# Transposed probabilities stored by 64-query halves: which engine copies what, and into which range

## The chip, the cores and the metric

The kernel runs on one core of one Trainium2 chip. The metric is the device time of one execution in microseconds. It is one hand-scheduled program that runs attention, a mixture-of-experts layer and a second feed-forward layer one after the other.

## The reference

Only the first part, attention, is touched by the change. Everything is float32; B = 2 batches, H = 8 heads, S = 576 positions, D = 64.

```python
scores = scale * np.matmul(q, k.transpose(0, 1, 3, 2))
...
scores = scores + bias.transpose(2, 0, 1)[None, :, :, :]   # a small network of the distance
scores = scores - np.max(scores, axis=-1, keepdims=True)
attn = np.exp(scores)
attn = attn / (np.sum(attn, axis=-1, keepdims=True) + 1e-09)
return np.matmul(attn, v).astype(np.float32)
...
x = np.ascontiguousarray(attn_out.transpose(0, 2, 1, 3)).reshape(B * S, H * D)
x = _moe_ref(x=x, **moe_kwargs)      # each token goes to one of 8 experts, weighted by its gate
return _moe2_ref(x=x, **moe2_kwargs) # 512 -> 2048 -> 512 with a leaky activation
```

## The kernel before, in words

**Units and slots.** Heads are taken in pairs `hp` (0 to 3). The 576 queries are cut into four blocks of 128 and a rest of 64. `SL` lists 24 slots: slots 0 to 3 hold the rests ("small" units) of batch 0, slots 4 to 11 one block each of batch 0, and from slot 12 on a slot holds a unit of two blocks (0 and 1, or 2 and 3) of one head pair; slots 12, 13, 18 and 20 hold a small unit of batch 1 besides. Slots 14 to 17 are batch 0, blocks 2 and 3; slot 18 begins the second half of batch 1. Slot 24 only finishes slot 23's unit.

**The course.** Slot s computes the scores of its own unit u = SL[s] and finishes the unit w = SL[s - 1] of the slot before. TensorE, ScalarE and VectorE follow the order in which `course` writes their instructions. SyncE's transfers (SP) are ordered by a scheduler, each as early as its buffer comes free. For two-block units the order is: scores of u's first block (TensorE, L253); `low`, which adds the bias, takes the minimum of the negated sum and writes it to SBUF (VectorE, L260, twice, one per head); the transposes of w's probabilities (`turn`, L290) with their copies to SBUF; the exponentials of u's first block (`expo`, ScalarE, L267, one per head, each followed by a read of its accumulator); scores and `low` of u's second block; if the slot before held a small unit, that one's transposes; `values`, the products with the values (L330, and L332 for the last 64 keys); the exponentials of the second block; the copy of the products to `xT` (VectorE, L334).

**Transposes and copies.** Nine column groups j of 128 hold the two heads' 1152 probabilities of a query: 0 to 3 for one head, 5 to 8 for the other, 4 the last 64 of both. `turn(w, 4)`, `turn(w, 0, 1, 2, 3)` and `turn(w, 5, 6, 7, 8)` each transpose their groups into one PSUM tile of two banks: the two 64-query halves of a block go to bank 0 and bank 1 (TensorE works on both halves of its rows). The copy function that `turn` returns, called with `('A')`, lets ScalarE copy both banks (L274); with `('A', 'D')` ScalarE copies bank 0 and VectorE bank 1 (L276). Their target is the SBUF tile `PT` [128, 9, 256]: for each j, 256 columns ordered (block, half, query), so the two engines' 64-column runs alternate. Where two instructions of different engines write overlapping ranges of a tile, the second waits for the first. PSUM holds two such tiles of two banks ("pt", also used by `values`, `row` and the routing) and two for the scores ("pq"); a tile is written again only when its readers are done.

**`row`.** From slot 17 on, steps of the routing of batch 0 are woven in. `row(0, 1)` and `row(3, 4)` transpose two blocks of finished rows (L478) into one two-bank tile, multiply each by the reciprocal sums (VectorE, L488) and append its gate and index (L489); GpSimd then scatters them. The first row's transposes come first, then its multiplication, then the second row's. `row(2)` stands alone.

**After attention** (from about 193 us): the two feed-forward parts, TensorE's stream of matmuls on split float32 weights.

Of the kernel before, what the change touches and what calls it, by code (L numbers as in the profile page):

```python
# [10 lines left out]
F32 = mybir.dt.float32  # L11
# [10 lines left out]
B, H, S, D = 2, 8, 576, 64  # L22
# [17 lines left out]
def build(tc, nc, a):  # L40
    V, A, G, T, SY = nc.vector, nc.scalar, nc.gpsimd, nc.tensor, nc.sync
    with contextlib.ExitStack() as ctx:
# [8 lines left out]
        ap = pool(left, "ap", 2)  # L51
# [5 lines left out]
        packed = True  # L57
        ps2 = lambda name: pt.tile([128, 2, 512], F32, tag="pt", name=name)

        def ps1(p, name):  # L60
            if packed:
                return ps2(name)[:, 0]
            return p.tile([128, 512], F32, tag="pt" if p is pt else "pa", name=name)
# [34 lines left out]
        ident = gp.tile([128, 128], F32, name="ident")  # L98
# [8 lines left out]
        xT = [xp.tile([128, 4, 640], F32, tag=f"xT{b}", name=f"xT{b}") for b in range(B)]  # L107
# [123 lines left out]
        halfs = [slice(64 * h, 64 * h + 64) for h in range(2)]  # L231
# [32 lines left out]
        def expo(u, ul=0, h=0):  # L264

            out, mn, acc = u.sc[ul, h]
            A.activation(out, out, AF.Exp, bias=mn, scale=-1.0, accum_out=acc)  # L267
            if u.small:
                u.dup = ap.tile([128, 2, 64], F32, tag="dup", name="dup", bufs=2)
                G.tensor_copy(u.dup, u.P[:, 512:576].unsqueeze(1).to_broadcast([128, 2, 64]))  # L270
# [7 lines left out]
        def turn(u, *js):  # L278

            t = ps2("t1")  # L280
            if u.small:
                u.PT = ap.tile([128, 5, 128], F32, tag="pt4", name="pt4", bufs=2)
                rows = [u.P[:, 128 * j:128 * j + 128] for j in range(4)] + [u.dup.rearrange("p a b -> p (a b)")]
            else:
                if js[0] == u.first:
                    u.PT = ap.tile([128, 9, 256], F32, tag="PT", name="PT")
                rows = [u.P[ul][:, 128 * j:128 * j + 128] for j in js for ul in u.uls]
            for i, x in enumerate(rows):
                for h, p in enumerate(halfs):
                    T.transpose(t[:, h, 64 * i:64 * i + 64], x[p], ident[p, p])  # L290
            src = t[:, :, 0:64 * len(rows)].rearrange("p h (m c) -> p h m c", c=64)
            if u.small:
                def out():
                    copy('A', u.PT[:, 0:4].rearrange("p m (h c) -> p h m c", h=2), src[:, :, 0:4])
                    for h, p in enumerate(halfs):
                        copy('D', u.PT[p, 4, 0:64], src[p, h, 4])
                return out
            dst = u.PT[:, js[0]:js[-1] + 1, :128 * len(u.uls)]
            if len(u.uls) == 2:
                dst = dst.rearrange("p j (i h c) -> p h (j i) c", h=2, c=64)  # L300
            else:
                dst = dst.rearrange("p j (h c) -> p h j c", h=2)

            def out(*es):
                if len(es) == 1:
                    copy(es[0], dst, src)
                else:
                    for h, e in enumerate(es):
                        copy(e, dst[:, h], src[:, h])
            return out  # L310

        def values(*us):
            o = ps1(pa, "av")
            outs, at = [], 0
            for u in us:
                v = u.v
                if u.small:
                    n, dst = 64, xT[u.b][:, u.hp, 512:576]
                    rhs = lambda h, j: u.PT[:, j, 64 * h:64 * h + 64]
                    rest = u.PT[:, 4, 0:64]  # L320
                else:
                    n, q0 = 128 * len(u.uls), 128 * u.uls[0]
                    dst = xT[u.b][:, u.hp, q0:q0 + n]
                    rhs = lambda h, j: u.PT[:, 5 * h + j, :n]
                    rest = u.PT[:, 4, :n]
                c = slice(at, at + n)
                at += n
                for j in range(4):
                    for h, p in enumerate(halfs):
                        T.matmul(o[p, c], v[:, j, p], rhs(h, j), start=j == 0, stop=False, skip_group_check=True)  # L330
                for p in halfs:
                    T.matmul(o[p, c], vd[u.b][:, u.hp, p], rest, start=False, stop=True, skip_group_check=True)  # L332
                outs.append((dst, o[:, c]))
            return lambda: [V.tensor_copy(*z) for z in outs]  # L334

        def first(f):
# [31 lines left out]
        def routing(b):  # L368
# [100 lines left out]

            def row(*us):  # L470
                t = ps2("xp") if packed else ps1(pt, "xp")
                for i, u in enumerate(us):
                    x = r.x[u] = raw.tile([128, RW], F32, tag="xr", name="xr", bufs=5)
                    if packed:
                        c = 256 * i
                        for hp in range(4):
                            for h, p in enumerate(halfs):
                                T.transpose(t[:, h, c + 64 * hp:c + 64 * hp + 64], xT[b][p, hp, 128 * u:128 * u + 128],  # L478
                                            ident[p, p])
                        z = x[:, 0:DM].rearrange("p (g h d) -> p h g d", h=2, d=64)  # L480
                        y = t[:, :, c:c + 256].rearrange("p h (g d) -> p h g d", d=64)
                        w = r.rinv[:, u].rearrange("p (g h) -> p h g", h=2).unsqueeze(3).to_broadcast([128, 2, 4, 64])
                    else:
                        for hp in range(4):
                            T.transpose(t[:, 128 * hp:128 * hp + 128], xT[b][:, hp, 128 * u:128 * u + 128], ident)
                        z, y = [z.rearrange("p (h d) -> p h d", h=8) for z in (x[:, 0:DM], t)]
                        w = r.rinv[:, u].unsqueeze(2).to_broadcast([128, 8, 64])
                    V.tensor_tensor(z, y, w, ALU.mult)  # L488
                    V.tensor_copy(x[:, DM:RW], r.gt[:, u])  # L489
# [428 lines left out]
        def course():  # L918
# [51 lines left out]
            for s in range(NU + 1):  # L970
# [11 lines left out]
                if u is None or len(u.uls) == 2:  # L982
# [3 lines left out]
                        low(u, u.uls[0], 1)  # L986
                    if len(w.uls) == 2:
                        turn(w, 4)('A')
                        if u:
                            expo(u, u.uls[0], 0)  # L990
                        turn(w, 0, 1, 2, 3)('A', 'D')
                        turn(w, 5, 6, 7, 8)('A', 'D')
                    else:
                        turn(w, 0, 1, 2, 3, 4)('A')
                        expo(u, u.uls[0], 0)
                        turn(w, 5, 6, 7, 8)('A')
                    if u:
                        scores(u, u.uls[1])
                        expo(u, u.uls[0], 1)
                        low(u, u.uls[1], 0)  # L1000
                        low(u, u.uls[1], 1)
# [246 lines left out]
```

## Time and profile before

| | us |
|---|---|
| time before, median of 3 runs | 386.43 (385.21 to 387.69) |
| profiled execution, its own time | 386.03 |
| its span, first to last instruction | 384.1 |
| TensorE matmuls busy | 351.6 |
| VectorE busy | 279.3 |
| ScalarE busy | 233.6 |
| first and last start of VectorE's copies to PT (L276) | 92.8, 186.7 |

The table's busy times are unions over the whole span; TensorE's is modelled, since its matmuls are pipelined. Times in rows of the trace are from the span's start. A row "x8" stands for eight instructions merged; a bracket gives the engine's idle time just before and what ended it.

### The profile page before, as it was taken

The page shows a single profiled execution, that of the slowest core. Times are in us where ns is not written, and L with a number is a line of the kernel's source. Part 1 is how long each engine was busy: PE and PEld are TensorE (multiplying, and loading weights), DVE is VectorE, ACT ScalarE, POOL GpSimd, SP SyncE. Part 2 cuts the span into 40 slices and gives each one's busy share as a digit, 9 for nine tenths or more (in the row PEclk, how much of TensorE's full clock was granted, in tenths as well). Part 3 has the DMA queues.
Part 4 walks back from the last instruction along what each step waited for, and adds up shares of the span by engine and source line. Part 5 has one row for each costly group of instructions (what it writes and reads, how often), then busy time and mean ns, then how long its engine had stood idle before and what let it go on. Part 6 is the DMA issues. An engine that isn't in the chain of part 4 may idle for free. (4 is left out here: it accounts for less than half of the span.)

```text
span 384.1 us, 8342 instructions
## 1 busy us (share of the span) xinstructions
PE 351.6 (92%) x3132; PEld 264.0 (69%) x3133; DVE 279.3 (73%) x679; ACT 233.6 (61%) x518; POOL 29.2 (8%) x48
## 2 busy tenths in 40 slices
PE   4988999999999998888799979999999999999992
PEld 2423565666666656565479979778988989887881
DVE  5988977846656656877589996048999999678430
ACT  4877899987656654555663446236776675555531
POOL 2000000000000000023013330020000000000013
PEclk9999999999999999999999999999999999999997
DMA  8897987999999940610883695863566556340003
GB/s 317 226 302 258 381 276 245 295 287 342 335 375 388 390 183 20 215 57 18 276 220 119 185 300 189 265 199 95 159 190 182 173 178 180 118 132 2 1 0 136
DMA packets 44013, 78.82 MB, mean 205 GB/s; under 512 B 7127, under 2 KB 21591, under 8 KB 43964
## 3 DMA queue, kind: packets, MB, share of 16 engines
q1 hardware_dynamic: 42780, 75.73, 61.0%
q0 software_dynamic: 1184, 2.48, 1.8%
q8 instruction: 26, 0.43, 0.5%
q14 instruction: 23, 0.19, 0.1%
HBM read 59.50 MB, written 20.09 MB: 207 GB/s over the span
## 5 line engine op out<-in xcount | busy, mean ns | idle before, releaser
L267 ACT ACTIVATE p<-p,mn 128x576 f32<-128x576 f32 x72 | 56.0, 778 | 20.2 <-DVE mn L260 20.2
L260 DVE CUSTOM_DVE_ANT_0 p<-sps,bias 128x576 f32<-128x576 f32 x72 | 51.9, 754 | 19.3 <-PE sps L253 12.0
L253 PE MATMUL sps<-kqv 64*128 64x288 f32 x256 | 50.7, 429 | 2.5 <-DVE mn L260 1.9
L176 DVE TENSOR_SCALAR h<-c 128x528 f32<-128x528 f32 (+17 forms) x126 | 46.5, 445 | 0.2
L184 PE MATMUL bps<-h,c 128*32 128x512 f32 (+17 forms) x352 | 36.5, 503 | 7.6 <-DVE h L176 5.2
L253 PEld LDWEIGHTS sps<-kqv 64*128 64x128 f32 x256 | 28.3, 186 | 15.8 <-DVE mn L260 5.0
L274 ACT COPY PT<-t 128x512 f32<-128x512 f32 (+2 forms) x52 | 26.8, 549 | 19.4 <-PE t L290 19.4
L330 PE MATMUL av<-PT,kqv 128*64 128x256 f32 (+1 forms) x320 | 35.5, 344 | 2.1 <-DVE PT L276 1.2
L851 PE MATMUL fg<-yh,w1l 128*128 128x304 f32 x120 | 36.3, 302 | 0.0
L851 PE MATMUL fg<-yh,w1h 128*128 128x304 f32 x120 | 36.2, 302 | 0.0
L851 PE MATMUL fg<-yl,w1h 128*128 128x304 f32 x120 | 36.2, 302 | 0.0
L290 PEld LDWEIGHTS t<-ident,p 64*128 64x128 f32 x640 | 28.9, 139 | 10.5 <-DVE PT L276 2.7
L290 PE MATMUL t<-ident,p 64*128 64x64 f32 x640 | 32.9, 227 | 2.9 <-DVE xT L334 1.2
L192 ACT ACTIVATE st<-bps,c 128x527 f32<-128x527 f32 (+35 forms) x72 | 31.1, 510 | 4.4 <-PE bps L184 4.4
L776 ACT ACTIVATE cv<-d 128x512 f32<-128x512 f32 x32 | 21.6, 674 | 19.7 <-DMA d<-in_wout 11.2
L330 PEld LDWEIGHTS av<-PT,kqv 128*64 128x64 f32 x320 | 20.8, 136 | 17.7 <-DVE PT L276 6.4
L863 PE MATMUL facc<-w2h,hl 128*128 128x512 f32 (+1 forms) x75 | 30.1, 401 | 0.3 <-DVE hl L547 0.3
L863 PE MATMUL facc<-w2h,hh 128*128 128x512 f32 (+1 forms) x75 | 29.8, 397 | 0.4 <-ACT hh L546 0.3
L863 PE MATMUL facc<-w2l,hh 128*128 128x512 f32 (+1 forms) x75 | 29.6, 394 | 0.0
L184 PEld LDWEIGHTS bps<-h,c 128*32 128x32 f32 x352 | 12.2, 115 | 23.6 <-DVE mn L260 8.9
L546 ACT CAST hh<-g 128x304 fp32r<-128x304 f32 x32 | 14.3, 445 | 15.9 <-DVE g L855 15.9
L851 PEld LDWEIGHTS fg<-yh,w1h 128*128 128x128 f32 x120 | 22.6, 188 | 1.0
(200 smaller groups left out, 735.2 us busy)
## 6 DMA issues: line engine op xcount, KB each, us to landing
bias<-bd SPq DMA_DIRECT2D x24, 576.0 KB, 6.5
kqv<-in_kqv SPq DMA_DIRECT2D x14, 864.0 KB, 7.7
bd<-st SPq DMA_DIRECT2D x36, 295.5 KB, 6.3
raw<-in_ew SPq DMA_DIRECT2D x16, 512.0 KB, 6.5
d<-in_win SPq DMA_DIRECT2D x16, 512.0 KB, 3.9
d<-in_wout SPq DMA_DIRECT2D x16, 512.0 KB, 3.5
w<-in_ew SPq DMA_DIRECT2D x6, 512.0 KB, 8.4
xd<-zr SPq DMA_DIRECT2D x4, 722.8 KB, 12.4
```

The lines of the kernel that those rows point to most:

```text
L176: V.tensor_scalar(h, tab[:, :n], psi[:, i:i + 1], 0.0, ALU.add, ALU.max)
L184: T.matmul(ps[32 * c:32 * c + 32, n0:n1], w2n, hs[c][:, n0:n1], start=True, stop=True)
L192: A.activation(st[:, o:o + src.shape[1]], src, AF.Copy, scale=rr[:, t:t + 1])
L253: T.matmul(u.sc[ul, h][0][:, nh, :288], q[p, 128 * ul:128 * ul + 128], k[p, 288 * nh:288 * nh + 288], start=True, stop=True)
L260: V.tensor_tensor_reduce(out.rearrange("p (a b) -> p a b", a=2), ps[:, :, :288], bias.rearrange("p (a b) -> p a b", a=2), -0.125, 3.0e38, ...
L267: A.activation(out, out, AF.Exp, bias=mn, scale=-1.0, accum_out=acc)
L274: A.copy(o, i)
L290: T.transpose(t[:, h, 64 * i:64 * i + 64], x[p], ident[p, p])
L330: T.matmul(o[p, c], v[:, j, p], rhs(h, j), start=j == 0, stop=False, skip_group_check=True)
L776: A.mul(v, r[:, :, 1].bitcast(F32), 2.0 ** -112)
L851: T.matmul(ps, w[:, 128 * k:128 * k + 128], x[:, k, s], start=k + i == 0, stop=k + i == 5)
L863: T.matmul(acc[i][:m], h[:, r:r + m], w, start=f == 0 and j == 0, stop=f == NF - 1 and j == 2)
```

## The change

1. `PT` becomes [128, 2, 9, 128]: half first, then j, then (block, query). Each half's copy fills a range of its own.
2. `values` reads its moving operand as two pieces, one per half; its output columns come in the order (half, block, query), and the copy to `xT` puts them back.
3. In two-block slots the copy of groups 0 to 3 goes to ScalarE whole instead of being split, and the first exponential moves behind all the copies. In slot 12 (one-block w) the exponential moves behind the second copy.
4. In `row`, the transposes of both rows come before both multiplications.

```diff
--- before.py
+++ after.py
@@ -283,7 +283,7 @@
                 rows = [u.P[:, 128 * j:128 * j + 128] for j in range(4)] + [u.dup.rearrange("p a b -> p (a b)")]
             else:
                 if js[0] == u.first:
-                    u.PT = ap.tile([128, 9, 256], F32, tag="PT", name="PT")
+                    u.PT = ap.tile([128, 2, 9, 128], F32, tag="PT", name="PT")
                 rows = [u.P[ul][:, 128 * j:128 * j + 128] for j in js for ul in u.uls]
             for i, x in enumerate(rows):
                 for h, p in enumerate(halfs):
@@ -295,11 +295,8 @@
                     for h, p in enumerate(halfs):
                         copy('D', u.PT[p, 4, 0:64], src[p, h, 4])
                 return out
-            dst = u.PT[:, js[0]:js[-1] + 1, :128 * len(u.uls)]
-            if len(u.uls) == 2:
-                dst = dst.rearrange("p j (i h c) -> p h (j i) c", h=2, c=64)
-            else:
-                dst = dst.rearrange("p j (h c) -> p h j c", h=2)
+            dst = u.PT[:, :, js[0]:js[-1] + 1, :64 * len(u.uls)]
+            src = src.rearrange("p h (j i) c -> p h j (i c)", i=len(u.uls))
 
             def out(*es):
                 if len(es) == 1:
@@ -321,8 +318,8 @@
                 else:
                     n, q0 = 128 * len(u.uls), 128 * u.uls[0]
                     dst = xT[u.b][:, u.hp, q0:q0 + n]
-                    rhs = lambda h, j: u.PT[:, 5 * h + j, :n]
-                    rest = u.PT[:, 4, :n]
+                    rhs = lambda h, j: u.PT[:, :, 5 * h + j, :n // 2]
+                    rest = u.PT[:, :, 4, :n // 2]
                 c = slice(at, at + n)
                 at += n
                 for j in range(4):
@@ -330,7 +327,11 @@
                         T.matmul(o[p, c], v[:, j, p], rhs(h, j), start=j == 0, stop=False, skip_group_check=True)
                 for p in halfs:
                     T.matmul(o[p, c], vd[u.b][:, u.hp, p], rest, start=False, stop=True, skip_group_check=True)
-                outs.append((dst, o[:, c]))
+                y = o[:, c]
+                if not u.small:
+                    y, dst = [z.rearrange(r, c=64, i=len(u.uls))
+                              for z, r in ((y, "p (h i c) -> p h i c"), (dst, "p (i h c) -> p h i c"))]
+                outs.append((dst, y))
             return lambda: [V.tensor_copy(*z) for z in outs]
 
         def first(f):
@@ -469,16 +470,17 @@
 
             def row(*us):
                 t = ps2("xp") if packed else ps1(pt, "xp")
+                if packed:
+                    for i, u in enumerate(us):
+                        for hp in range(4):
+                            for h, p in enumerate(halfs):
+                                c = 256 * i + 64 * hp
+                                T.transpose(t[:, h, c:c + 64], xT[b][p, hp, 128 * u:128 * u + 128], ident[p, p])
                 for i, u in enumerate(us):
                     x = r.x[u] = raw.tile([128, RW], F32, tag="xr", name="xr", bufs=5)
                     if packed:
-                        c = 256 * i
-                        for hp in range(4):
-                            for h, p in enumerate(halfs):
-                                T.transpose(t[:, h, c + 64 * hp:c + 64 * hp + 64], xT[b][p, hp, 128 * u:128 * u + 128],
-                                            ident[p, p])
                         z = x[:, 0:DM].rearrange("p (g h d) -> p h g d", h=2, d=64)
-                        y = t[:, :, c:c + 256].rearrange("p h (g d) -> p h g d", d=64)
+                        y = t[:, :, 256 * i:256 * i + 256].rearrange("p h (g d) -> p h g d", d=64)
                         w = r.rinv[:, u].rearrange("p (g h) -> p h g", h=2).unsqueeze(3).to_broadcast([128, 2, 4, 64])
                     else:
                         for hp in range(4):
@@ -986,15 +988,13 @@
                         low(u, u.uls[0], 1)
                     if len(w.uls) == 2:
                         turn(w, 4)('A')
-                        if u:
-                            expo(u, u.uls[0], 0)
-                        turn(w, 0, 1, 2, 3)('A', 'D')
+                        turn(w, 0, 1, 2, 3)('A')
                         turn(w, 5, 6, 7, 8)('A', 'D')
                     else:
                         turn(w, 0, 1, 2, 3, 4)('A')
-                        expo(u, u.uls[0], 0)
                         turn(w, 5, 6, 7, 8)('A')
                     if u:
+                        expo(u, u.uls[0], 0)
                         scores(u, u.uls[1])
                         expo(u, u.uls[0], 1)
                         low(u, u.uls[1], 0)
```

## Rows read from the trace of the kernel before

**Rows 1.** The page's busy time, share of the span and instructions, TensorE.

```profile
PE 351.6 (92%) x3132; PEld 264.0 (69%) x3133; DVE 279.3 (73%) x679; ACT 233.6 (61%) x518; POOL 29.2 (8%) x48
```

**Rows 2.** Waits, 88 to 192 us: engine, line, waited for: us, times, longest.

```profile
DVE PT L276 <- ACT PT L274: 8.8, 12, 0.8
...
PEld av L330 <- DVE PT L276: 6.4, 14, 0.7
```

**Rows 3.** Timeline around a `row` pair: start, us, engine, line, operation.

```profile
167.60 0.33 PEld L478 LDWEIGHTS xp<-ident,xT 64*128 64x128 f32 x8 [1.00 <-DVE xr L488]
...
169.13 0.76 DVE L260 CUSTOM_DVE_ANT_0 p<-sps,bias 128x576 f32<-128x576 f32 x1
```

**Rows 4.** Timeline of a plain slot (16, from 113.61) and the next starts.

```profile
114.69 1.47 PE L290 MATMUL t<-ident,p 64*128 64x64 f32 x36
...
115.01 0.37 ACT L274 COPY PT<-t 128x256 f32<-128x256 f32 x1 [1.36 <-PE t L290]
...
115.57 0.75 DVE L260 CUSTOM_DVE_ANT_0 p<-sps,bias 128x576 f32<-128x576 f32 x1
...
115.75 0.78 ACT L267 ACTIVATE p<-p,mn 128x576 f32<-128x576 f32 x1 [0.36 <-DVE mn L260]
...
115.99 1.63 PE L253 MATMUL sps<-kqv 64*128 64x288 f32 x8
...
116.52 1.05 ACT L274 COPY PT<-t 128x512 f32<-128x512 f32 x2
...
117.12 1.29 DVE L276 COPY PT<-t 128x512 f32<-128x512 f32 x2 [0.79 <-ACT PT L274]
...
117.87 2.32 PE L330 MATMUL av<-PT,kqv 128*64 128x256 f32 x15 [0.25 <-DVE PT L276]
...
118.46 1.27 PEld L330 LDWEIGHTS av<-PT,kqv 128*64 128x64 f32 x13 [0.41 <-DVE PT L276]
...
119.95 0.76 ACT L267 ACTIVATE p<-p,mn 128x576 f32<-128x576 f32 x1
...
120.03 0.80 PE L332 MATMUL av<-PT,vd 128*64 128x256 f32 x3
...
120.76 0.79 PEld L253 LDWEIGHTS sps<-kqv 64*128 64x128 f32 x8 [0.38 <-issue]
...
127.92 0.79 PEld L253 LDWEIGHTS sps<-kqv 64*128 64x128 f32 x8 [0.39 <-issue]
```

**Rows 5.** Groups by shape: count, busy us, mean ns, idle before.

```profile
L274 ACT COPY PT<-t 128x512 f32<-128x512 f32 x32 | 17.4, 580 | 0.8 <-PE t L290 0.8
...
L276 DVE COPY PT<-t 128x512 f32<-128x512 f32 x24 | 15.5, 686 | 8.8 <-ACT PT L274 8.8
...
L274 ACT COPY PT<-t 128x640 f32<-128x640 f32 x8 | 5.5, 694 | 4.0 <-PE t L290 4.0
```

**Rows 6.** Timeline of slot 14, which has a small unit to finish.

```profile
102.98 0.33 PEld L290 LDWEIGHTS t<-ident,p 64*128 64x128 f32 x8 [0.68 <-DVE PT L276]
103.58 1.95 PE L330 MATMUL av<-PT,kqv 128*64 128x256 f32 x16
105.36 0.60 PE L332 MATMUL av<-PT,vd 128*64 128x256 f32 x4
```

**Rows 7.** Timeline, products of a one-block unit.

```profile
75.40 1.09 PE L330 MATMUL av<-PT,kqv 128*64 128x128 f32 x16
```

**Rows 8.** Timeline, slots 19 and 24.

```profile
145.18 1.52 PEld L330 LDWEIGHTS av<-PT,kqv 128*64 128x64 f32 x16 [0.59 <-ACT p L267]
...
186.80 0.36 PEld L599 LDWEIGHTS xjT<-ident,xj 96*128 96x128 f32 x4 [1.04 <-DVE PT L276]
```

**Rows 9.** Windows: busy us (x) of each engine, clock, DMA share, GB/s.

```profile
86.00:140.00 54.00, 51.52 (x564) 33.31 (x565) 32.37 (x86) 34.41 (x83) 1.22 (x5) 1.00 1.00 360
140.00:150.00 10.00, 9.17 (x131) 7.30 (x127) 7.10 (x22) 5.08 (x12) 0.22 (x1) 1.00 0.01 2
```

**Rows 10.** DMA issues within 113.2 to 113.6: KB, us to landing.

```profile
kqv<-in_kqv SPq DMA_DIRECT2D x1, 864.0 KB, 12.1
```

## The prediction

> **What bounds the kernel now.** I began with the busy line of the page: TensorE is busy 92% of the span, the next engine far less [rows 1], so time is won where TensorE stands still, or streams behind a wait. The view of waits, cut to the stretch of the two-block units, names who makes it wait: the products with the values (L330) wait for VectorE's copies of the transposed probabilities (L276) 14 times, 6.4 us; those copies had themselves waited 12 times, 8.8 us, for ScalarE's copy of the other half [rows 2]. Twice, the transposes of `row` wait for the multiplication of the row before, L488 [rows 3]. Then I read one plain slot in order of time [rows 4]; the reader should lay its rows side by side. VectorE ends the last `low` of the first block at 116.33 (115.57 + 0.75, plus 0.08 to read the accumulator) and is idle until 117.12, which is when ScalarE's first copy ends (116.52 + about 0.58 [rows 5]). The two copies fill different 64-column groups of one range, and have different source banks; nothing else links them. ScalarE in turn spent 115.75 to 116.52 on an exponential that nobody needs before the next slot. So PT is full only at 118.41, the scores of the second block have ended at 117.62, two weight loads of L330 go at 117.87, and the other eighteen of its and L332's twenty from 118.46. The slot lasts 7.15 us (113.61 to 120.76, 120.76 to 127.92 [rows 4]).
>
> **Part 1: the copies of j = 0 to 3 go to ScalarE whole, ahead of the exponential.** A plain slot, step by step. The 36 transposes start at 114.69 and end at 116.16, about 0.04 us each; the twentieth, the last that this copy needs, ends near 115.5. ScalarE is free of the j = 4 copy at 115.38. The trace has no 1024-element copy; 512 elements take 0.580 and 640 take 0.694 us [rows 5], 0.89 ns per element, which gives 1.04 us; its bounds are 0.94 (two copies back to back take 1.05 [rows 4], so the second adds 0.47; twice that) and 1.16 (two whole ones). So it runs 115.55 to 116.6, and ScalarE's half of j = 5 to 8 ends near 117.1. VectorE's only copy, its half of j = 5 to 8, starts when `low` is done and its transposes are: 116.4 to 117.1. PT is full at 117.1 instead of 118.41, before the scores of the second block end at 117.62. What is late next is TensorE itself: L330 starts when those scores have ended. At the other boundary of the slot the same is seen: the last L332 product ends at 120.83 and the first weight load of the next scores goes at 120.76, after 0.38 us in which nothing was waited for [rows 4]. I take 117.55 for the first weight load. Uninterrupted, the twenty products take 2.38 us (103.58 to 105.96, in a slot where they start with everything ready [rows 6]), so they end at 119.93 instead of 120.83: **0.9 us**. If instead the eighteen keep the pace that they have now after the wait, 0.7. I take 0.8.
>
> The Trainium skill, TensorEngine Tiling (Array Packing), section Key Properties, says that changing the tiling mode drains TensorE. The trace agrees as far as those two rows go. Were there no drain, the saving per plain slot would be larger by about that gap, 0.38 us.
>
> Two costs of the move. ScalarE does about 0.45 us more copying per slot, and the first exponential ends 1.2 us later (near 118.0 instead of 116.5). It is covered so: four exponentials at a pitch of 0.77 after 117.0 would end at 120.1, and the third can't start before its `low` ends near 118.4 (VectorE is free, the scores end at 117.62), so the last ends at 120.1 to 120.2, against 120.71 now (119.95 + 0.76 [rows 4]); the next slot's transposes need it 0.84 us after a start at 119.95, at 120.8. The cover is 0.6 us; without it each slot loses what is missing. VectorE loses a 0.686 us copy [rows 5], and its `low`s of the second block start when their scores end, earlier than now.
>
> **Part 2: layout.** Copies keep their element counts. The 512-element copies of today write runs of 64 and cost what the element counts say, so runs of 64 in the copy of `av` to xT cost nothing. The products read their moving operand in two pieces (128 + 128 columns, 64 + 64 for one-block units), which no row shows. Sixteen products of 128 columns take 1.09 us [rows 7], sixteen of 256 take 1.95 [rows 6]: 0.068 and 0.122 each, so a product in two pieces that each cost what a product of 128 costs would be 0.014 us longer, 3.4 us for 20 products of twelve units: the upper end. The lower is nothing, since the same columns are read; that excludes a gain too. I take 0.
>
> **Part 3: slots with a small unit or routing.** In slots 13, 14 and 21 the small unit's transposes stand before L330 and wait, in slot 14 until 102.98, for the j = 0 to 3 copies [rows 6]. Now they follow the scores directly (102.3, the buffer free at 102.2), and L330 starts near 102.9 instead of 103.58: 0.65 us. Slot 19: L330 starts at 145.18 when the small unit's copies have freed its accumulator [rows 8]; VectorE reaches them 0.7 earlier, but ScalarE's part of them now comes behind two exponentials, which leaves 0.5. Slot 24: the transposes of job rows wait for VectorE's copies until 186.80 [rows 8]; ScalarE's whole copy ends near 186.45, and the chain behind gains 0.3. Slot 20 (the rank products go first) and 22 (a `row` goes first) lie between 0 and 0.8; I take 0.3 and 0.45.
>
> **Part 4: `row`.** Twice, TensorE stands 1.00 us for the first row's multiplication before the second row's transposes [rows 3]. Now sixteen transposes run on and the next scores start 0.9 us sooner, but both multiplications (0.69 each) still precede the slot's first `low` on VectorE, which now starts at 169.13 [rows 3] and could start near 168.45: 0.7 us each, 1.4.
>
> **Part 5: what the loads allow.** From 86 to 140 us the DMA engines are busy throughout, 360 GB/s [rows 9]: transfers land one behind the other, and issuing them sooner brings none forward. The one that matters is slot 18's kqv, issued within 113.2 to 113.6 and landing 12.1 us later [rows 10], at about 125.4; slot 18 starts at 127.92 [rows 4]. So no more than 2.5 us of the gain can be had before slot 18, though slots 13 to 17 would give 0.65 + 0.65 + 3 x 0.8 = 3.7 (slot 12, whose exponential moves too, would only add to what is cut). After slot 18 starts, the DMA engines soon run dry (busy 0.01 of 140 to 150 [rows 9]), and nothing is held up.
>
> **Sum.** 2.5 + slot 18 0.8 + slot 19 0.5 + slot 20 0.3 + slot 21 0.65 + `row` 1.4 + slot 22 0.45 + slot 23 0.8 + slot 24 0.3 = **7.7 us**. What follows slot 24 is TensorE's stream, which starts that much sooner; the job rows' loads follow the last `row`, which itself comes some 6 us sooner. The profiled execution took 386.03 (span 384.1 and 1.9 around it), 0.4 under the median of 386.43; taken from the median: **378.7 us**.
>
> **The rivals.**
> A. ScalarE becomes the late engine. For it: all moved work lands on it, and behind slot 14, whose small copies come after two exponentials, I work out a cover of only 0.25 us. Against it: four exponentials at 0.77 and copies of 0.37 and 1.05 [rows 4] fill about 4.5 of 7.15 us of a plain slot. If its chain lets a slot gain only 0.3 instead of 0.65 to 0.8, the gain is 7 slots after the cap at 0.3, 1.5 before it, and `row`: 5.0 us, 381.4. The Trainium skill, TensorEngine Tiling (Array Packing), section PSUM Bottleneck, advises to use both ScalarE and VectorE for emptying PSUM, which speaks against this part. Here VectorE's half couldn't have started before 116.4 and would have ended no sooner than ScalarE's whole copy.
> B. The change doesn't do what it says: VectorE's remaining copy still waits for ScalarE's. Against: its range (second half, j = 5 to 8) lies behind all that ScalarE writes. If it waited, PT would be full at 117.8, L330 would start 0.25 later, and the sum would lose 0.25 x 8: 5.7 us, 380.7.
> C. The loads become the bound and the kernel slower. SP's order is not written out by hand, and what is placed ahead of slot 18's kqv delays it: each 768 KB fill of out by 2.2 us at 360 GB/s [rows 9], each bias load (576 KB) by 1.6. The slots behind give 5.2, so it ends slower once that kqv lands 7.7 us later (2.5 + 5.2): three fills and two biases, 9.8, give 388.5. One fill gives 380.9. For it: the saturated queue. Against: the loads' order follows when buffers come free, and all of these come free sooner alike.
> D. TensorE's stops are covered elsewhere (the routing's chain on VectorE, the job's weights), and only what is on the chain in plain slots is won: under 3 us, 383.5 to 386.
>
> **How the numbers follow.** My forecast, with 376.3 to 380.7 from the bounds (0.9 per plain slot and a cap less tight at one end, 0.7 and nothing from slots 20, 22 and 24 at the other), 0.58; A or B 0.2; D 0.13; C 0.09, half of it faster still. The range must leave out no more than 0.2: 375.8 to 383.2. A difference of 1%, 3.9 us, is about what a measurement of this kernel tells from none (382.6 and 390.3). Faster by over 1%: the forecast, most of A and B, a little of C, 0.77. Within: 0.18. Slower: 0.05.
>
> **What would show it.** In the profile after: L276 half as many 512-element copies (12) and no wait of theirs for L274; a 1024-element L274 copy near 1.04 us; in a plain slot L330's weight loads in one run right behind the scores, slot length 6.3 to 6.5; slot 18's first scores waiting for a DMA; no wait of L478 for L488. It is wrong if L330's products take longer than 2.4 us, if transposes wait for exponentials, or if the loads come in another order.

## The result, and the profile after

The changed kernel takes 382.36 us (median of 20 runs, 379.29 to 385.58), the kernel before in the same rounds 386.85 (383.63 to 389.26): ratio 0.9879, 95% interval 0.9852 to 0.9907. It is faster by 1.2%, 4.5 us, within the range; the forecast was 7.7 us. Here and below a median is over all runs of a kernel, and a ratio leaves out those in a slower state of the chip. The profiled execution took 384.18 us with a span of 382.3, only 1.8 below the one before; why that is less is told below.

The page's first line for TensorE, and the granted clock over 40 slices of the span:

```profile
PE 351.3 (92%) x3132; PEld 266.5 (70%) x3133; DVE 271.8 (71%) x667; ACT 237.8 (62%) x518; POOL 28.7 (8%) x48
...
PEclk9999999999999999999699999999999999999999
```

TensorE is as busy as before [rows 1]. The view of waits of the changed kernel, 88 to 192 us (us in total, times, longest):

```profile
DVE PT L276 <- ACT PT L274: 11.2, 12, 1.2
...
PE sps L253 <- DMA kqv<-in_kqv: 2.3, 2, 1.7
PEld av L327 <- DVE PT L276: 2.0, 5, 0.4
```

Here is the first surprise. The wait of VectorE's copy for ScalarE's copy, which the separate ranges were to end, is still there at all twelve copies, and longer: 11.2 us in all against 8.8 [rows 2]. What it costs TensorE has fallen from 6.4 to 2.0 us. Two waits for kqv loads are new. Now the plain slot of [rows 4], slot 16, in order of time, with the start of slot 15 ahead of it:

```profile
105.12 0.54 PEld L253 LDWEIGHTS sps<-kqv 64*128 64x128 f32 x6
...
111.60 0.79 PEld L253 LDWEIGHTS sps<-kqv 64*128 64x128 f32 x8 [0.38 <-issue]
...
113.00 2.00 ACT L274 COPY PT<-t 128x256 f32<-128x256 f32 x3 [1.36 <-PE t L290]
...
113.56 0.76 DVE L260 CUSTOM_DVE_ANT_0 p<-sps,bias 128x576 f32<-128x576 f32 x1
...
115.03 0.69 DVE L276 COPY PT<-t 128x512 f32<-128x512 f32 x1 [0.72 <-ACT PT L274]
115.54 1.51 PEld L327 LDWEIGHTS av<-PT,kqv 128*64 128x64 f32 x15 [0.38 <-issue]
115.54 1.97 PE L327 MATMUL av<-PT,kqv 128*64 128x256 f32 x15
```

From 105.12 to 111.60, slot 15 lasts 6.48 us instead of 7.15. In slot 16 ScalarE's three copies run through from 113.00 to 115.00. VectorE's `low` ends at 114.3, but its copy starts at 115.03, when ScalarE's last one ends. The products go in one run behind the scores, with 0.38 us in which nothing was waited for. In a slot with a small unit the scores end earlier against the copies, and the wait shows; slot 14 of [rows 6], and below it one of the two `row` pairs of [rows 3]:

```profile
101.49 0.69 DVE L276 COPY PT<-t 128x512 f32<-128x512 f32 x1 [1.17 <-ACT PT L274]
...
102.23 1.49 PEld L327 LDWEIGHTS av<-PT,kqv 128*64 128x64 f32 x16 [0.45 <-DVE PT L276]
...
163.99 0.71 PE L478 MATMUL xp<-ident,xT 64*128 64x64 f32 x16
...
166.09 0.75 DVE L260 CUSTOM_DVE_ANT_0 p<-sps,bias 128x576 f32<-128x576 f32 x1
```

`row`'s sixteen transposes now run on. Last, the starts of slots 17 and 18 and the products of slot 24:

```profile
118.81 1.24 PE L253 MATMUL sps<-kqv 64*128 64x288 f32 x8 [0.66 <-DMA kqv<-in_kqv]
...
126.98 0.82 PEld L253 LDWEIGHTS sps<-kqv 64*128 64x128 f32 x8 [2.08 <-issue]
127.02 1.24 PE L253 MATMUL sps<-kqv 64*128 64x288 f32 x8 [1.66 <-DMA kqv<-in_kqv]
...
185.31 3.68 PE L327 MATMUL av<-PT,kqv 128*64 128x256 f32 x16 [0.52 <-DVE xl L549]
```

Slots 17 and 18 stand for their loads, 0.66 and 1.66 us, though slot 18 starts only 0.94 us sooner than before (127.92 [rows 4]). The sixteen products of slot 24 took 1.95 us in the kernel before; here the clock was granted at 0.50 from 184 to 188 us, 1.2 GHz.

**Where the time went, as one table.** Take the start of VectorE's first `low` of a slot in a run, less its start in the kernel before; then subtract the same difference at slot 12 (83.22 in the kernel before, 82.75 in the changed one). That leaves out what differs ahead of the changed part. In the kernel before, the first `low` of slot 15 starts at 107.74, of slot 18 at 129.19, of slot 22 at 169.13, and the first one of slot 23's second block at 181.22. Gains in us; the first line is the sum of the prediction's own terms up to there (half of slot 23's), in brackets without the cap for the loads:

| | slot 15 | slot 18 | slot 22 | slot 23 | median, us |
|---|---|---|---|---|---|
| predicted | 1.3 | 2.5 (3.7) | 5.45 (6.65) | 7.0 (8.2) | 378.7 |
| the change | 0.88 | 0.47 | 2.58 | 4.02 | 382.36 |
| e1, the same again | 0.87 | 2.89 | 5.01 | 4.46 | 382.59 |
| e2, old layout | 0.87 | 1.68 | 3.79 | 3.23 | 382.14 |
| e3, no wait | 1.54 | 1.73 | 4.47 | 5.15 | 381.13 |
| e4, fills held | 0.88 | 2.89 | 5.03 | 4.45 | 380.89 |
| e5, no wait, fills held | 1.54 | 3.97 | 6.72 | 9.01 | 376.48 |
| e6, before, no wait | 1.15 | 3.06 | 5.34 | 6.78 | 379.17 |
| e7, before, row | 0.01 | 0.02 | 0.79 | 1.48 | 384.71 |
| e8, before, fills held | 0.00 | 0.00 | 0.02 | 0.02 | 385.57 |
| e9, before, all three | 1.14 | 3.30 | 6.33 | 6.84 | 378.78 |
| e10, e5 with both copies shared | 1.54 | 3.69 | 6.59 | 7.14 | 380.24 |
| e11, exponential first | -0.64 | -1.58 | -1.91 | -2.71 | 390.19 |
| e12, e5 in the old layout | 1.54 | 3.97 | 6.70 | 7.25 | 381.38 |

Slot 12 itself gives 0.40 where its exponential was moved (0 in e6, e7 and e9), on which the prediction counted only as something that the cap would take. The kernel before, run beside e1 to e4, e5 to e8 and e9 to e12, had medians of 386.40, 386.07 and 386.19.

### The profile page after: what moved, and what is told of

Read it like the earlier page. It is cut to its first block, busy times and chain, and to the rows that moved or that the text cites. A ratio compares the mean times of both kernels' runs of the same rounds, so it can differ in the third digit from the quotient of the medians.

```text
span 382.3 us, 8335 instructions
## 1 busy us (share of the span) xinstructions
PE 351.3 (92%) x3132; PEld 266.5 (70%) x3133; DVE 271.8 (71%) x667; ACT 237.8 (62%) x518; POOL 28.7 (8%) x48
## 5 line engine op out<-in xcount | busy, mean ns | idle before, releaser
L260 DVE CUSTOM_DVE_ANT_0 p<-sps,bias 128x576 f32<-128x576 f32 x72 | 51.8, 753 | 22.4 <-PE sps L253 15.4
L267 ACT ACTIVATE p<-p,mn 128x576 f32<-128x576 f32 x72 | 55.8, 780 | 10.8 <-DVE mn L260 10.8
L253 PE MATMUL sps<-kqv 64*128 64x288 f32 x256 | 51.5, 430 | 4.8 <-DMA kqv<-in_kqv 2.3
L274 ACT COPY PT<-t 128x512 f32<-128x512 f32 (+3 forms) x52 | 31.8, 653 | 21.3 <-PE t L290 20.3
L253 PEld LDWEIGHTS sps<-kqv 64*128 64x128 f32 x256 | 28.7, 186 | 18.7 <-ACT st L192 5.3
L327 PE MATMUL av<-PT,kqv 128*64 128x256 f32 (+1 forms) x320 | 35.4, 356 | 2.1 <-DVE PT L276 1.1
L290 PEld LDWEIGHTS t<-ident,p 64*128 64x128 f32 x640 | 29.6, 139 | 8.6 <-issue 1.7
L290 PE MATMUL t<-ident,p 64*128 64x64 f32 x640 | 33.2, 226 | 2.3 <-ACT PT L274 0.8
L327 PEld LDWEIGHTS av<-PT,kqv 128*64 128x64 f32 x320 | 21.9, 141 | 15.5 <-ACT PT L274 5.5
```

The lines of the kernel that those rows point to most:

```text
L253: T.matmul(u.sc[ul, h][0][:, nh, :288], q[p, 128 * ul:128 * ul + 128], k[p, 288 * nh:288 * nh + 288], start=True, stop=True)
L260: V.tensor_tensor_reduce(out.rearrange("p (a b) -> p a b", a=2), ps[:, :, :288], bias.rearrange("p (a b) -> p a b", a=2), -0.125, 3.0e38, ...
L274: A.copy(o, i)
```

## The experiments

My theory after the first trace: VectorE's copy waits for ScalarE's because both read one PSUM tile, whatever ranges they fill; that wait and slot 18's load are what the gain was lost to. The rivals: the ranges do matter, or the loads and the clock stretch are chance. In the experiments some lines have moved: L275, L282 and L283 are L276, L281 is L274 (the copies); L329 is L330, L333 and L334 are L327 (the products); L258 is L253 (the scores), L267 in rows of VectorE is L260 (`low`), L296 is L290 (the transposes of the probabilities) and L477 is L478 (those of `row`).

**e1, the changed kernel once more.** No edit.

> The changed kernel once more, unaltered. Two things of its first trace are to be told apart from chance: TensorE granted half its clock from 182.5 to 189.3 us (the sixteen products of slot 24 took 3.68 us), and the loads of the kqv tiles of slots 17 and 18 landing at 118.67 and 126.88 us, 0.9 and 1.5 later than in the kernel before. Theory (both are chance of one execution): no half-clock stretch in slot 24, the sixteen products there take 1.9 to 2.0 us, slot 18 starts at 125.5 to 126, and the span is 378 to 380. Rival (both follow from the change): the same half-clock stretch between 180 and 190 and the same landings within 0.3 us, span 382.

382.59 us, 0.9893 (0.9839 to 0.9946). Slot 18 starts without a wait:

```profile
125.09 0.79 PEld L253 LDWEIGHTS sps<-kqv 64*128 64x128 f32 x8 [0.39 <-issue]
```

Its kqv, issued at 111.80, landed at 124.52; in the first trace it was issued at 112.30 and landed at 126.88, 14.6 us later, against 12.1 [rows 10]. So the late landing is chance, and so are the 2.4 us that it and slot 17's cost; e2 and e3 waited there again (1.1 us in e2). The half clock did come back, 0.58 to 0.50 in the 2 us windows from 184 to 190, so there the theory failed for this kernel. Its span is 381.1 us, not the 378 to 380 of the theory: slots 22 and 23, which gained 1.44 us in the first trace, lost 0.55 here (5.01 to 4.46 in the table). Yet ten of the fourteen traces of this case have such a stretch between 178 and 198 us, e8's among them, whose code there is the kernel before's; the traces of before, e2, e4 and e12 have none. TensorE's busy time ahead of it hardly tells them apart: 4.76 of the 6 us from 176 to 182 in the trace of the change, 4.43 in e4's. Between what stands at 182.6 and at 191.5 in the trace of before, e8 loses 1.39 us, and between 183.7 and 191.5 the changed kernel loses 2.64. The trace of before was thus one without that loss, which is why the two profiled executions differ by so little; its clock over the 40 slices:

```profile
PEclk9999999999999999999999999999999999999997
```

The mean clocks of all runs are close: median 0.990 (26 runs of the change), 0.988 (51 of before).

**e2, the layout alone put back.**

```diff
-u.PT = ap.tile([128, 2, 9, 128], F32, tag="PT", name="PT")
+u.PT = ap.tile([128, 9, 256], F32, tag="PT", name="PT")
...
-rhs = lambda h, j: u.PT[:, :, 5 * h + j, :n // 2]
+rhs = lambda h, j: u.PT[:, 5 * h + j, :n]
...
-outs.append((dst, y))
+outs.append((dst, o[:, c]))
```

> The changed kernel with only the layout of the transposed probabilities put back (one range of 9 x 256, products with one moving operand of 256 columns, the copy of the results without regrouping). Theory (the layout does nothing, because the wait of VectorE's copy for ScalarE's comes from both reading one PSUM tile): within 0.3% of the changed kernel, VectorE's 512-element copy waits for ScalarE's as before, 0.7 us in a plain slot in both, sixteen products of 256 columns 1.95 us in both. Rival 1 (the separate ranges free VectorE's copy): without them the products of slots 13 to 24 start 0.3 to 0.5 later each, 3 to 5 us slower than the changed kernel. Rival 2 (a moving operand in two pieces costs): 3.4 us faster than the changed kernel.

382.14 us, 0.9874 (0.9819 to 0.9929): the same. VectorE's copy waits for ScalarE's 12.7 us in all in e1 and in e2 alike, and fifteen products in a row take 1.97 us in both layouts (e2's row is the first, e1's the second):

```profile
116.02 1.97 PE L330 MATMUL av<-PT,kqv 128*64 128x256 f32 x15
```

```profile
122.55 1.97 PE L327 MATMUL av<-PT,kqv 128*64 128x256 f32 x15
```

So the layout neither frees the copy nor costs TensorE anything.

**e3, the wait taken away.** The two copies read different banks and fill different ranges, so the second needn't follow the first:

```diff
-for h, e in enumerate(es):
-    copy(e, dst[:, h], src[:, h])
+x, y = [copy(e, dst[:, h], src[:, h]) for h, e in enumerate(es)]
+tc.declare_no_dep(y.ins, x.ins, reason="two banks, two ranges")
```

> The changed kernel, with VectorE's copy of its half of j = 5 to 8 declared independent of ScalarE's copy of the other half (other PSUM bank, other range of the destination). Theory (that wait is what holds slots 13, 14, 19 and 21 to 24 back): no wait for ScalarE at that copy; the products no longer wait 0.35 to 0.45 us for it in those slots and the transposes of job rows in slot 24 not 0.85; what is won before slot 18 is taken back by its load, so 0.45 (slot 19) + 0.4 (21) + 0.36 (22) + 0.35 (23) + 0.6 (24), some 1.5 to 2.2 us faster than the changed kernel; the plain slots 15 to 17 keep 6.48. Rival (ScalarE's copy ends as late anyhow): 0 to 0.3 us.

381.13 us, 0.9802 (0.9730 to 0.9874). By slot 15 it has won 1.54 instead of 0.88 us, by slot 16's second block 3.39 instead of 2.22. Then slots 17 and 18 wait 1.00 and 1.17 us for their kqv, slot 18's landed at 125.91, and most of that is gone. That the loads would take it was expected. Of the terms expected behind them slot 19's 0.45 didn't come (its gain is 0.17 to 0.18 in e1 and e3 alike), slot 21's 0.4 did (1.36 against 0.97 up to slot 22). The plain slots did better than expected, about 6.35 instead of 6.48. The median is 1.5 us under e1's, but the two intervals overlap.

**e4, the fills of zeros held.** They wait for slot 18's first scores, and are issued from slot 19 on:

```diff
+i = SY.dma_start(xd[:].rearrange("(p r) w -> p r w", r=12)[:, r:r + 3],
+                 zr[0:n].unsqueeze(1).to_broadcast([n, 3, RW]))
+rows_of.wait(i.ins, HOLD)
...
+if u is SL[18][-1] and ul == u.uls[0]:
+    HOLD.append(i.ins)
...
-LD[s].append((clear, 3 * s - 51))
+LD[max(s, 19)].append((clear, 3 * s - 51))
```

> The changed kernel with the seven fills of zeros (four of xd, three of out) held until slot 18's scores have started, so that they stand behind the loads that slots 17 to 19 need. Theory (the loads' queue takes the gain of slots 13 to 17 back): slots 17 and 18 wait for no DMA, slot 18 starts near 124.2 to 124.8 us against 126.98, and the kernel is 2 to 3 us faster than the changed one. Rival (the loads are late because their buffers come free late, not because of what stands ahead): landings move less than 1 us and the time less than 0.7. A second rival: the fills now come beside the job's weights after 140 us and delay them; the time is the same or slower, with TensorE waiting for a DMA between 170 and 200.

380.89 us, 0.9850 (0.9800 to 0.9900), 1.7 us under e1, where 2 to 3 were expected; the intervals overlap. Slot 18's kqv now lands 6.1 us after its issue, at 116.93, and nothing waits for a load. The second row shows slot 24 at full clock:

```profile
124.11 0.79 PEld L258 LDWEIGHTS sps<-kqv 64*128 64x128 f32 x8 [0.38 <-issue]
...
184.08 1.95 PE L334 MATMUL av<-PT,kqv 128*64 128x256 f32 x16 [0.66 <-DVE xl L556]
```

Up to slot 22 e4 and e1 agree to 0.02 us in the table: e1 was an execution in which the loads happened to be in time, and the hold gives what the loads take in the others (the first trace, e2, e3).

**e5, both edits.**

> The changed kernel with both edits: VectorE's copy independent of ScalarE's, and the fills of zeros held until slot 18 has started. Theory (these two are what the change's gain was lost to): no wait of VectorE's copy for ScalarE's, no wait of slots 17 and 18 for a DMA, every slot from 13 to 18 shorter than in the kernel before by 0.55 to 0.85, the lows of slot 19 earlier by 4.5 to 5.0 us than at slot 12, and 377.5 to 379.5 in all, 7 to 9 below the kernel before. Rival (with these waits gone another takes their place, the exponentials before the transposes or a buffer's release): slots of 6.4 to 6.5 us still, and no better than with the fills held alone, 380 to 381.

376.48 us, 0.9750 (0.9697 to 0.9804), the fastest kernel of this case, 1 us under what was expected (but see e12). Its plain slot lasts 6.34 us. VectorE's copy runs beside ScalarE's; the row of 112.17 is the middle one of ScalarE's three copies:

```profile
110.27 0.79 PEld L258 LDWEIGHTS sps<-kqv 64*128 64x128 f32 x8 [0.38 <-issue]
...
111.66 2.00 ACT L281 COPY PT<-t 128x256 f32<-128x256 f32 x3 [1.22 <-PE t L296]
...
112.17 1.01 ACT L281 COPY PT<-t 128x1024 f32<-128x1024 f32 x1
...
112.32 0.75 DVE L267 CUSTOM_DVE_ANT_0 p<-sps,bias 128x576 f32<-128x576 f32 x1
...
112.99 0.69 DVE L282 COPY PT<-t 128x512 f32<-128x512 f32 x1
...
114.30 1.49 PEld L333 LDWEIGHTS av<-PT,kqv 128*64 128x64 f32 x16 [0.38 <-issue]
...
116.61 0.79 PEld L258 LDWEIGHTS sps<-kqv 64*128 64x128 f32 x8 [0.38 <-issue]
```

These rows also answer whether the two copies were linked by the target tile as a whole: VectorE's starts at 112.99, while ScalarE still writes other columns of the same `PT`, until 113.18, out of another PSUM tile. Only the dependency on the copy that shares the PSUM tile was dropped.

The gain at slot 22 is 6.72; less the 0.40 of slot 12 that is 6.32, where the prediction without its cap has 6.65.

**e6, the kernel before with the wait alone taken away** (the same two lines as e3, in the old layout and order).

> The kernel before with one edit: at both copies that are shared, VectorE's half is declared independent of ScalarE's; layout, order and assignment stay. Theory (the wait was never one of ranges, so the old layout runs without it too): VectorE's two copies run from the end of its low, 116.4 to 117.8 in the plain slot of the rows, the products go in one run behind their first two weight loads, plain slots are shorter by 0.5 to 0.65, and slot 18 comes 2 to 2.5 us sooner and waits for its load; 2 to 3.5 us faster in all. Rival (the change's own order, one engine for the first copy and the exponential behind, is needed): 0 to 0.7 us.

379.17 us, 0.9816 (0.9766 to 0.9865): one declaration gives more than the whole change. I had expected 2 to 3.5 us. The plain slot lasts 6.43:

```profile
113.11 1.24 PE L253 MATMUL sps<-kqv 64*128 64x288 f32 x8
...
115.84 1.28 DVE L275 COPY PT<-t 128x512 f32<-128x512 f32 x2
...
116.06 1.05 ACT L274 COPY PT<-t 128x512 f32<-128x512 f32 x2
...
117.14 1.58 PEld L329 LDWEIGHTS av<-PT,kqv 128*64 128x64 f32 x16 [0.39 <-ACT PT L274]
...
119.54 0.79 PEld L253 LDWEIGHTS sps<-kqv 64*128 64x128 f32 x8 [0.38 <-issue]
```

Both engines' pairs end at the same time, 117.1, where VectorE's alone ended at 118.41 [rows 4].

**e7, the kernel before with only `row` changed.**

> The kernel before with only the second part of the change: in row both rows' transposes ahead of the products. Theory: TensorE's two waits of 1.00 us for a product of row are gone, the next slot's lows come 0.7 earlier each time, 1.4 us faster in all, which is at the edge of what the timing tells; the trace shows the two steps of 0.7 at slots 22 and 24. Rival (VectorE's two products are the longer way and the time returns at the next slot's transposes): 0 to 0.3.

384.71 us, 0.9972 (0.9941 to 1.0003). The timing hardly tells it from nothing; the trace does: 0.77 at slot 22 and 0.69 more behind, 1.46 in all.

```profile
165.82 0.71 PE L477 MATMUL xp<-ident,xT 64*128 64x64 f32 x16
...
167.91 0.75 DVE L260 CUSTOM_DVE_ANT_0 p<-sps,bias 128x576 f32<-128x576 f32 x1
```

**e8, the kernel before with the fills held** (e4's edit).

> The kernel before with the fills of zeros held until slot 18 has started, and nothing else. Theory (before the change the loads were not late): slots 12 to 18 start at the same distances as before, 7.15 us for a plain slot, the loads of slots 17 and 18 land 5 us or more ahead of their use, time the same within 0.3%. Rival (the saturated queue slows other things too, or the fills beside the later loads cost): a change of more than 1 us either way.

385.57 us, 1.0003 (0.9967 to 1.0039); every `low` from slot 12 to 23 stands where it stood, to 0.02 us. Before the change the loads were no bound; the change made them one.

**e9, the kernel before with e6's, e7's and e8's edits.**

> The kernel before (old layout, old order, copies shared as they were) with the three edits that have been tried one by one: VectorE's halves independent of ScalarE's, row's transposes ahead of its products, the fills of zeros held. Theory (with the wait gone, who copies what matters little): slot 24's lows 8 to 9 us sooner relative to slot 12 (6.8 measured with the first edit alone, 1.5 with the second, some lost to the load of slot 18), plain slots 6.3 to 6.45 us, 376.5 to 378.5 in all. Rival (the change's order of copies and exponential is worth something of its own even so): 1 us or more above the 376.5 of the changed kernel with the same edits.

378.78 us, 0.9795 (0.9754 to 0.9835). By the table it is 0.39 under e5 at slot 22, all of it there at slot 15 already and due to slot 12: once the wait is gone, the new order of copies and exponential gives nothing more by then. By the median it is 2.3 us above e5, so the rival's bound was met; most of that lies behind slot 22, see e12.

**e10, e5 with groups 0 to 3 shared again.**

```diff
-turn(w, 0, 1, 2, 3)('A')
+turn(w, 0, 1, 2, 3)('A', 'D')
```

> The changed kernel with the wait removed and the fills held, and the copy of j = 0 to 3 shared again between ScalarE and VectorE (exponential still behind the copies). Theory (two engines don't empty the tile sooner, since VectorE comes to it only when its lows are done): VectorE's two copies end 0.6 to 0.7 us later than its one, plain slots longer by 0.1 to 0.25, 1 to 2 us above the 376.5 of the same kernel with ScalarE copying j = 0 to 3 whole. Rival (sharing is better once there is no wait): 375 to 376.

380.24 us, 0.9836 (0.9798 to 0.9873). Up to slot 22 sharing costs 0.13 us, less than expected; the median is 3.8 above e5, more than expected, and again most of it from behind slot 22.

The Trainium skill, TensorEngine Tiling (Array Packing), section PSUM Bottleneck, advises both engines for emptying PSUM. In these slots the trace shows no gain from it: 6.59 against 6.72 us.

**e11, the change with the first exponential put back ahead of the copies.**

```diff
 turn(w, 4)('A')
+if u:
+    expo(u, u.uls[0], 0)
 turn(w, 0, 1, 2, 3)('A')
 turn(w, 5, 6, 7, 8)('A', 'D')
...
 if u:
-    expo(u, u.uls[0], 0)
     scores(u, u.uls[1])
```

> The changed kernel with one step put back: the first exponential again ahead of the copy of j = 0 to 3, the wait and the fills as the change has them. Theory (the order is the part that gains, the assignment alone loses): ScalarE's copies run 116.5 to 118.0 in the plain slot of the rows, VectorE's waits for them and ends near 118.7, the products come 0.3 later than in the kernel before; with 1.5 us from row and no gain in slot 12, 386 to 389, 1 us or more above the kernel before or even with it. Rival (VectorE's freed time is what gains): 382 to 384, as the change.

390.19 us, 1.0073 (1.0038 to 1.0108): slower than before, by more than expected. A plain slot lasts 7.46 us (114.40 to 121.86), 0.31 more than before:

```profile
117.31 1.48 ACT L274 COPY PT<-t 128x1024 f32<-128x1024 f32 x2
...
118.82 0.69 DVE L276 COPY PT<-t 128x512 f32<-128x512 f32 x1 [1.70 <-ACT PT L274]
...
119.56 1.27 PEld L327 LDWEIGHTS av<-PT,kqv 128*64 128x64 f32 x13 [1.02 <-DVE PT L276]
```

So of the change's copy part the assignment alone loses, since VectorE's copy waits for all of ScalarE's, and moving the exponential out of that chain wins 0.98 us per plain slot (7.46 to 6.48).

**e12, e5 in the old layout** (e2's edit).

> The changed kernel with the wait removed and the fills held, in the old layout. Theory (the layout does nothing): 376.5 within 1 us, plain slots 6.34, no wait of VectorE's copy for ScalarE's. Rival (without the wait the layout shows: the products' moving operand in one piece or two, the copies' runs of 64): 1.5 us or more either way.

381.38 us, 0.9849 (0.9816 to 0.9883), 4.9 above e5, on the rival's side by the timing. By the trace it isn't the layout where the layout works: from slot 12 to slot 22 the two agree to 0.02 us, plain slot for plain slot. The spans differ by 4.8. Of that 2.9 stand at slot 12 already (its first `low` at 85.19 against 82.31), with a half-clock stretch at 32 to 36 us in e12 and not in e5, and 1.7 come in slots 22 and 23. There ScalarE's copy starts at 166.19, 1.63 behind the first of its transposes (164.56); in e5 at 162.42, 0.75 behind (161.67):

```profile
164.56 1.22 PE L296 MATMUL t<-ident,p 64*128 64x64 f32 x32 [0.41 <-DVE xr L496]
...
166.19 1.50 ACT L281 COPY PT<-t 128x1024 f32<-128x1024 f32 x2 [1.62 <-PE t L296]
```

```profile
161.67 1.22 PE L296 MATMUL t<-ident,p 64*128 64x64 f32 x32 [0.41 <-DVE xr L497]
...
162.42 1.50 ACT L281 COPY PT<-t 128x1024 f32<-128x1024 f32 x2 [0.74 <-PE t L296]
```

The rows name TensorE's transposes as what ScalarE waited for. The ends of matmuls are modelled, so no row shows whether the transposes ended late or only the word of it came late. And six runs of e12, all above all six of e5, are more than one trace can explain. There is a rival that no run settles: e5 was timed with e6 to e8 on one chip, e9 to e12 later on another, and e5 never beside them. The kernel before agrees in both (386.07 and 386.19), but this standstill is in the traces of e9, e10 and e12, as in those of e1 to e4 on a third chip, and in none of e5 to e8. So this stays open; 376.5 is what e5 measured, not all of it is the sum of its parts, and how much of its lead over e9, e10 and e12 belongs to the kernel is not shown beyond slot 22.

## Why the prediction was right, and what in it was wrong

Faster by over 1% came true and the range held the time, 0.8 us from its upper end, but the forecast was 3.7 us too low: two of its steps failed, and slots 22 and 23 lost what no step foresaw. The layout, from which I expected the freed copy, gave nothing (e2). What gained was the exponential's place behind the copies (e11) and `row` (e7). So the way was right for a part of its reasons, and that the range held is partly luck.

**Part 1, "nothing else links them", failed.** I held that the two copies wait for each other because their target ranges interleave, and that VectorE's only copy would start when its `low` is done. The source links them: both read one PSUM tile. By e1 and e2 the wait is the same in either layout, so the rule of overlapping ranges, told ahead of the prediction, isn't what makes it in the changed kernel; by e5's rows it isn't the target tile as a whole; in e3, e5, e6 and e12 it is gone in either layout, once that one dependency is dropped. Rival B was thus true, and my argument against it (its range lies behind all that ScalarE writes) was about the wrong tile. Its price was near as far as slot 22: I put 2 us on it, and e5 less e4 is 6.72 - 5.03 = 1.69 there, e12 less e4 1.67. But it is hardly paid where I put it, alike in eight slots: a plain slot loses 0.14 (6.48 against 6.34), while slots 13 and 14, where TensorE comes to the products early, gained 0.27 and 0.21 instead of 0.65 each (e5: 0.55 and 0.59). For the whole kernel the price is open: by the medians 4.4 us from e4 to e5, and none from e4 to e12.

The Trainium skill, PSUM — Partial Sum Buffer, section PSUM bank collisions raise a hardware error, says that accesses of two engines to one bank and quadrant must be kept apart, two reads as well. Two copies that only read it were kept apart here (12.7 us of waits in e1); but these two read different banks, so the wait was wider than that rule asks.

**Part 5, the cap of 2.5 us, was a fixed number for something that varies.** The landing of slot 18's kqv, forecast at 125.4, came at 126.88 and 124.52 in two executions of the same kernel, so the change keeps 0.47 or 2.89 us of its gain up to there. Rival C's mechanism, fills ahead of that load, is what makes it late: held back, they let it land at 116.93 (e4). They needn't move in the order for that; it was enough that TensorE came sooner (e8). Slot 17's load, which I left out, was late as well: 0.66 us in the first trace, 1.00 in e3.

**What held.** Part 1's plain slot: 0.67 with the wait and 0.81 without, for 0.8; the 1024-element copy takes 1.01 us, for 1.04; in the changed kernel no transposes wait for exponentials, so rival A didn't come (without the wait they do, twice, 0.8 us in e5). Part 2's zero: 1.97 us for fifteen products in both layouts. Part 4's 1.4: 1.46. Of part 3, slot 19 gave 0.16 in e4 and 0.18 in e5 instead of 0.5, wait or no wait: in e5 it wins 0.55 by its third `low`, of which 0.37 go again behind it, at the routing's steps, which is rival D in one slot. Slot 20 gave 0.32, for 0.3. Slot 21 gave 0.97 in e4 and 1.35 in e5; less 0.77 for `row` that is 0.20 with the wait and 0.58 without, for 0.65.

**Slots 22 and 23** were to give 1.55 us up to the table's last column (0.45, a `row` of 0.7, half of 0.8). They gave 1.44 in the first trace and 2.29 in e5, but -0.55 to -0.58 in e1, e2 and e4. e1, which lost nothing to loads, stood at 5.01 of 5.45 at slot 22 and at 4.46 of 7.0 in the last column: of the 2.5 that it lacks, 2.1 are lost in these two slots. What stands still there is told in the last section; its cause is open.

**What follows slot 24** was forecast to start as much sooner. In the trace of the change 2.6 of its 4.5 us there were lost in the half-clock stretch. The trace of before happened to have none, nor that of e4, which kept its whole gain (5.36 us at slot 23, slot 12's start included, and 5.4 in the span). The medians over many runs hold both kinds for both kernels.

## What to carry to other kernels

A wait between two engines has a source tile and a target tile; before you change the layout to end it, name which of the two it is, and test by dropping that one dependency, which here gave 1.8% without the change. When a stretch is shortened under a busy DMA queue, look at what stands ahead of the next load that has to be in time: work that could go later, such as fills, costs nothing until the compute comes sooner. And weigh a rival by its price as well as by its chance: B was priced about right up to slot 22 and given too little, though one declaration would have tested it.

## What was not expected of the hardware

TensorE's clock was granted at half for 2 to 8 us at a time: near the end in all fourteen traces, between 178 and 198 us in ten, between 28 and 38 in four (e2, e6, e8, e12) and between 220 and 226 in two (e10, e12), whichever kernel ran. Where it was worked out, one stretch goes with a loss of 1.4 (e8) and 2.6 us (the change), as much as a third of the 7.7 us of the forecast.

ScalarE stood in front of a copy whose transposes had ended by the modelled rows, in slot 22 or 23 of e1, e2, e3, e4, e9, e10 and e12: gaps of 0.28 to 0.99 us between two copies that elsewhere follow with 0.1 or none, or the 0.88 of e12's rows. The trace of the change and e5 to e8 have none. Up to slot 23's second block this goes with some 2 us: slots 22 and 23 together give -0.55 to -0.58 in e1, e2 and e4 against 1.44 in the first trace, and, without the wait, 0.51 to 0.68 in e3, e9, e10 and e12 against 2.29 in e5. Why it comes in some executions is not shown.
